# One period of 162 named steps, laid out in another order: a gated recurrent attention with a feed-forward layer on one core

## The chip, the core and the metric

The kernel runs on one core of a Trainium2 chip, in one launch. The metric is the device time of that launch in microseconds, from runs on the chip. A core has five engines with an instruction stream each, which run side by side and wait for one another by semaphores: PE (TensorE, matmuls into the accumulators called PSUM; its weight loads are listed apart, as PEld), DVE (VectorE), ACT (ScalarE), POOL (GpSimd) and SP (SyncE), which in this kernel only issues DMAs.

## The reference

There are two parts. The first is a gated linear attention, for 4 batches, 8 heads, 768 tokens and 40 channels a head; the loop over tokens carries a state C (40 by 40 per head), a row n and a running maximum m:

```
m_new = max(f[t] + m, i[t])
C = exp(f[t] + m - m_new) * C + exp(i[t] - m_new) * outer(v[t], k[t])
n = exp(f[t] + m - m_new) * n + exp(i[t] - m_new) * k[t]
y[t] = sigmoid(o[t]) * (C q[t]) / max(|n . q[t]|, 1)
```

The second part takes y as 3072 rows of 320 numbers: `h = x @ w_in` (320 to 2048), `g = max(h, 0) + alpha * min(h, 0)` with an alpha per channel, and `g @ w_out` (2048 to 320), all in float32.

## The kernel before, in words

**Tiling.** Tokens go in chunks of 128: six chunks a batch, 24 in all, called n = 0 to 23; c is a chunk's place in its batch, 0 to 5. Two chunks make a group g = n // 2 of 256 tokens, 12 groups, three to a batch. Inside a chunk the attention is done in matrix form: scores of keys against queries, times decays (exponentials of gate sums, masked to the lower triangle), times values; plus the queries times the state left by earlier chunks of the batch. The state of a batch starts anew with its chunk c = 0. Hence chunk c = 0 has no term from the state, and c = 5 makes no update.

**Precision.** Float32 results come from matmuls on parts. In attention, q, k, v, the decayed scores and the state are each cut into bfloat16 parts (a high part, the rest, the rest of the rest). ACT makes the high part, POOL or DVE subtracts it. The parts of q and k are then transposed by two DMAs (`th`, `ti`), and four more DMAs stack them (`sh`, `shifted`, lines 279 to 282). In the feed-forward layer x, w_in, g and w_out are each a high and a low part in the chip's fp32r format.

**The feed-forward layer of a group** (`FeedForward`, from line 675) has eight rounds fp = 0 to 7 of 256 hidden channels. A round has these steps, in capitals or small letters for two variants of the same work:

- V (or U): the up projection, 16 matmuls on PE (lines 697 to 704) into one of two PSUM buffers `ph`;
- r (R): the relu of the negated sum, on ACT (L707), into one of three buffers `g`;
- s (S): two operations of DVE (L712) that add the sum from PSUM; after them the `ph` buffer is free (in the U variant, which one round of eight uses, only after K);
- g (G): the high part `gh`, on ACT (L721); N: the low part `gl`, on POOL (K: on DVE) (L723). There are three buffers of each;
- D: the down projection, 12 matmuls on PE (L734) into `po`, the first eight on `gh`, the last four on `gl`.

F opens a group's layer, Z copies `po` out (DVE) and stores it (SP). Ahead of them X transposes the attention's output on PE into two PSUM tiles, and xa, xb (ACT) and xd, xe (DVE) cut it into parts; xe frees the second of the tiles.

**The steps of a chunk n of the later kind** (`late_steps`, from line 442):

- ld (q, k; L99), lv (v of a group; L112), lL (rows of gate sums; L119), lG (the output gate of a whole batch, six loads, line 128; issued at the last chunk of the batch before): loads on SP;
- ta to tg: parts of q and k. ta is a memset and two ACT copies; tb (L260, tile qr) and tc (L260, tile kr) are POOL's first subtractions; td, tf are ACT copies; te, tg (L265, tile Z) POOL's second. th, ti: the DMA transposes. sh: the four stacking DMAs;
- va, vb, vc, vd: parts of v, ACT and POOL in turn;
- e0, e1: the decays of the even and the odd heads, four ACT exponentials each, and POOL's mask (L436). s0, s1: the scores on PE (L462); m, c, d, h, l (0 or 1): the decayed scores and their parts, on DVE, ACT, DVE, ACT, DVE;
- y0, y1: times values on PE (L361), q0, q1 the sums on DVE. pi: queries times state on PE (L386), pt, ad the sum on DVE;
- r (three small operations of DVE), og (POOL, L418), xn (DVE, L420), xp (POOL): denominator, gate, output. oa (ACT, tanh, line 132) and ob (DVE) open the gate of the two chunks of a group;
- wd (POOL, L161): weighed keys. ua: outer products on PE (L183); ub (POOL, L210) and uc (DVE): the state's decay and sum; ud, ue, uf, ug: its parts, ACT and POOL in turn; uh (two DMAs, L233 and L234, that read the tile cw) and ui (one DMA, L236): the parts stacked.

The tiles qr, kr and cw share one tag with two buffers. So a tc may write only when an earlier cw is free, and that is when the DMAs of its uh have landed. The attention's PSUM tiles (scores, sums, pi, ua, X) share two tags with two buffers each, given out in turn.

**What sets the order.** Two lists of names do. `ORDER` (414 names) covers the first two groups up to the second one's middle, and `PATTERN` (162 names) is a period that `in_full` (line 650) repeats for g = -2 to 14. In it `s0.1` stands for s0 of chunk 2g + 1, `X:-1` for X of group g - 1, `V4<<` for round 4 of group g - 2's feed-forward and `V0<` for round 0 of group g - 1's. A name that doesn't exist (ua of a chunk with c = 5, say) or that was given out before is skipped. So in one period PE, ACT, DVE, POOL and SP do the attention of one group and the feed-forward of the groups before it, interleaved. `pin` (line 880) ties every instruction to the one before it on its engine. Each engine, and SP's queue of DMAs too, thus goes strictly by the list, and a step that waits holds up everything behind it on its engine.

Of the kernel before, what the change touches and what calls it, by code (L numbers as in the profile page):

```python
# [17 lines left out]
def kernel(ctx: ExitStack, tc: tile.TileContext, q, k, v, i_gate, f_gate, o_gate, w_in, w_out, alpha, out):  # L18
# [576 lines left out]
    def first_stacks():  # L595
# [40 lines left out]
        U12 fm5 ft5 o5h sc51 wg51 v5 o7d R12 S12 ta5 D10 G11 K11 o6s o6x gr5 og3 gg5 G12 gx5 gg4 D11 K12 D12 i30h i30l  # L636
        gx4 U13 gp5 D02 tp0 do3 U06 o7s gp4 o5l o6j vp0 R13 tp1 g05 S13 G13 N05 K13 o7x o6h D13 vp1 o7j U07 tp2 tp3
        R06 S06 R07 x4 x5 xa5 xd5 D03 D04 D05 S07 o7h o7l G06 K06 o6l D06 xa4 xd4 G07 K07 D07 Z0"""
    PATTERN = """va.1 uc.0 tf.1 V4<< c0.0 m1.0 N2<< d0.0 tg.1 r4<< V5<< r.-1 s4<< D2<< vc.0 g3<< th.1 og.-1 c1.0 h0.0 wd.1 xn.-1 r5<<
        xp.-1 d1.0 l0.0 g4<< ld.2 U6<< ud.0 h1.0 N3<< R6<< s5<< X:-1 N4<< g5<< S6<< lG.-1 ta.2 ua.1 V7<< ue.0 uf.0  # L640
        xa:-1 lL.2 xb:-1 l1.0 ub.1 vd.0 uc.1 r7<< N5<< tb.2 D3<< xd:-1 D4<< xe:-1 ti.1 F< ug.0 uh.0 G6<< sh.1 s7<<
        oa.0 y0.0 ld.3 pi.0 ob.0 tc.2 K6<< q0.0 y1.0 V0< td.2 e0.1 vb.1 vc.1 D5<< te.2 g7<< wd.2 q1.0 V1< pt.0 ad.0
        e1.1 r.0 s0.1 N7<< s1.1 r0< D6<< s0< vd.1 va.2 ud.1 tf.2 r1< m0.1 g0< c0.1 ue.1 tg.2 uf.1 lL.3 ug.1 m1.1 D7<<
        s1< d0.1 c1.1 og.0 th.2 g1< h0.1 ti.2 d1.1 ui.0 ta.3 xn.0 uh.1 V2< l0.1 ui.1 V3< sh.2 tb.3 Z<< r2< lG.8 h1.1
        N0< s2< l1.1 g2< D0< y0.1 N1< q0.1 y1.1 e0.2 pi.1 q1.1 vb.2 r3< tc.3 e1.2 lv.4 s1.2 xp.0 s0.2 td.3 ua.2 pt.1
        te.3 ad.1 s3< D1< ub.2 m0.2"""

    TWINS = dict(zip("UVRrSsGgKN", "VUrRsSgGNK"))

    def in_full():  # L650
# [4 lines left out]
        for g in range(-2, NG + 3):  # L655
            for x in PATTERN.split():
                if ":" in x:
# [645 lines left out]
```

## Time and profile before

| what | value |
|---|---|
| median of 3 runs | 478.0 us (477.29 to 484.12) |
| profiled execution | 480.86 us, span 479.1 us |
| busy share of the span | PE 98%, PEld 95%, DVE 65%, ACT 65%, POOL 64% |
| mean granted clock of TensorE | 0.986 of full |
| HBM | 36.90 MB read, 4.03 MB written |

The span runs from the first instruction of the profiled execution to its last; the time of the execution has about 1.8 us around it. An engine is busy while one of its instructions runs; matmuls overlap, so their ends are modelled. In rows of waits, `A <- B` says that A stood idle until B had ended. In names of tiles, `kS` and `qS` are the stacks of k and q, `pS` the scores, `pu` the outer products, `pH` values, `pI` queries times state, `ph` and `po` the up and down projections. `PEq` or `SPq` is the sequencer of an engine, which issues DMAs.

### The profile page before, as it was taken

The page shows a single profiled execution, that of the slowest core. Times are in us where ns is not written, and L with a number is a line of the kernel's source. Part 1 is how long each engine was busy: PE and PEld are TensorE (multiplying, and loading weights), DVE is VectorE, ACT ScalarE, POOL GpSimd, SP SyncE. Part 2 cuts the span into 40 slices and gives each one's busy share as a digit, 9 for nine tenths or more (in the row PEclk, how much of TensorE's full clock was granted, in tenths as well). Part 3 has the DMA queues.
Part 4 walks back from the last instruction along what each step waited for, and adds up shares of the span by engine and source line. Part 5 has one row for each costly group of instructions (what it writes and reads, how often), then busy time and mean ns, then how long its engine had stood idle before and what let it go on. Part 6 is the DMA issues. An engine that isn't in the chain of part 4 may idle for free.

```text
span 479.1 us, 11833 instructions
## 1 busy us (share of the span) xinstructions
PE 468.7 (98%) x4442; PEld 455.8 (95%) x4442; DVE 311.2 (65%) x664; ACT 312.5 (65%) x716; POOL 307.8 (64%) x395
## 2 busy tenths in 40 slices
PE   8999999999999999999989999999989999999997
PEld 6899989999999999999979999999989999999997
DVE  3869998658776676676556666766576676654221
ACT  4969898667766767666748758658657757523322
POOL 8531774844978868666977777677888776614231
PEclk9969999999999999999989999999999999999999
DMA  9979994959465565559685458559877533000000
GB/s 184 219 160 236 257 250 120 193 101 194 97 154 138 101 152 137 141 100 173 142 185 111 92 131 166 96 127 168 152 143 152 101 104 77 1 29 0 29 1 27
DMA packets 173922, 61.60 MB, mean 129 GB/s; under 512 B 140154, under 2 KB 166122, under 8 KB 173866
## 3 DMA queue, kind: packets, MB, share of 16 engines
q1 hardware_dynamic: 173786, 60.75, 60.0%
q8 instruction: 35, 0.57, 0.5%
q14 instruction: 21, 0.17, 0.1%
q10 hardware_dynamic: 80, 0.11, 0.1%
HBM read 36.90 MB, written 4.03 MB: 85 GB/s over the span
## 4 chain that ended last, share of the span: by engine, by line
PE 78%; DVE 5%; POOL 5%; SPq 3%; ACT 3%; DMA 3%; issue 2%; POOLq 0%; DVEq 0%; ACTq 0%
PE po L734 29%; PE ph L697 4%; PE ph L703 4%; PE ph L700 4%; PE ph L699 4%; PE ph L698 4%; PE ph L702 4%; PE ph L704 4%; PE ph L701 4%; PE pS L462 3%; PE pH L361 2%; PE pH L322 2%; PE pu L183 2%; PE p L551 2%; PE pS L1033 2%
## 5 line engine op out<-in xcount | busy, mean ns | idle before, releaser
L723 POOL TENSOR_TENSOR gl<-g,gh 128x512 fp32r<-128x512 f32 x77 | 100.2, 1306 | 43.3 <-ACT gh L721 37.6
L734 PE MATMUL po<-OH,gh 128*128 128x320 f32 x368 | 112.0, 316 | 0.0
L707 ACT ACTIVATE g<-ph 128x512 f32<-128x512 f32 x96 | 57.0, 594 | 82.7 <-PE ph L704 76.8
L734 PE MATMUL po<-OL,gh 128*128 128x320 f32 x368 | 109.7, 310 | 0.0
L712 DVE SCALAR_TENSOR_TENSOR g<-g,oma,ph 128x256 f32<-128x256 f32 x156 | 67.7, 476 | 52.0 <-ACT g L707 51.9
L734 PEld LDWEIGHTS po<-OH,gh 128*128 128x128 f32 x368 | 69.5, 189 | 0.4
L734 PEld LDWEIGHTS po<-OL,gh 128*128 128x128 f32 x368 | 69.5, 189 | 0.1
L734 PE MATMUL po<-OH,gl 128*128 128x320 f32 x368 | 69.0, 308 | 0.0
L734 PEld LDWEIGHTS po<-OH,gl 128*128 128x128 f32 x368 | 57.9, 188 | 0.0
L697 PE MATMUL ph<-XH,WH 128*128 128x256 f32 x192 | 56.4, 294 | 0.7 <-ACT wo L803 0.7
L436 POOL TENSOR_SCALAR_AFFINE_SELECT E<-E 128x512 f32<-128x512 f32 x40 | 25.6, 639 | 48.0 <-ACT E L433 47.6
L348 ACT CAST E<-pS 128x512 bf16<-128x512 f32 x72 | 41.1, 585 | 20.9 <-DVE pS L345 20.8
L703 PE MATMUL ph<-XL,WH 128*128 128x256 f32 x192 | 54.3, 283 | 0.0
L700 PE MATMUL ph<-XH,WL 128*128 128x256 f32 x192 | 54.2, 283 | 0.0
L699 PE MATMUL ph<-XH,WL 128*128 128x256 f32 x192 | 54.2, 282 | 0.0
L702 PE MATMUL ph<-XL,WH 128*128 128x256 f32 x192 | 54.2, 282 | 0.0
L721 ACT CAST gh<-g 128x512 fp32r<-128x512 f32 x77 | 47.5, 619 | 10.1 <-DVE g L712 6.9
L698 PE MATMUL ph<-XH,WH 128*128 128x256 f32 x192 | 54.2, 282 | 0.0
L701 PE MATMUL ph<-X,W 128*128 128x256 f32 x192 | 53.5, 279 | 0.2 <-POOL W L829 0.2
L704 PE MATMUL ph<-X2L,W 128*128 128x256 f32 x192 | 53.4, 278 | 0.0
L433 ACT ACTIVATE E<-Lb,bT 128x128 f32<-128x128 f32 x160 | 51.0, 392 | 0.0
L366 DVE TENSOR_REDUCE S<-pH 128x168 f32<-128x504 f32 x36 | 23.4, 679 | 22.3 <-PE pH L361 22.3
(193 smaller groups left out, 1141.9 us busy)
## 6 DMA issues: line engine op xcount, KB each, us to landing
Lb<-L_d SPq DMA_DIRECT2D x20, 512.0 KB
wo<-in_moe_w_out_dram SPq DMA_DIRECT2D x8, 640.0 KB
wi<-in_moe_w_in_dram SPq DMA_DIRECT2D x8, 512.0 KB
qn<-in_q_dram SPq DMA_DIRECT2D x24, 160.0 KB
kn<-in_k_dram SPq DMA_DIRECT2D x24, 160.0 KB
va<-in_v_dram SPq DMA_DIRECT2D x24, 160.0 KB
og<-in_o_gate_dram SPq DMA_DIRECT2D x24, 160.0 KB
out_dram<-ob SPq DMA_DIRECT2D x11, 320.0 KB
```

The lines of the kernel that those rows point to most:

```text
L697: nc.tensor.matmul(dst, WH[half][:, 0, hs], XH[:, 0], start=True, stop=False)
L698: nc.tensor.matmul(dst, WH[half][:, 1, hs], XH[:, 1], start=False, stop=False)
L699: nc.tensor.matmul(dst, WL[half][:, 0, hs], XH[:, 0], start=False, stop=False)
L700: nc.tensor.matmul(dst, WL[half][:, 1, hs], XH[:, 1], start=False, stop=False)
L701: nc.tensor.matmul(dst, W2[:, fs], X2, start=False, stop=False)
L702: nc.tensor.matmul(dst, WH[half][:, 0, hs], XL[:, 0], start=False, stop=False)
L703: nc.tensor.matmul(dst, WH[half][:, 1, hs], XL[:, 1], start=False, stop=False)
L704: nc.tensor.matmul(dst, W2[:, fs], X2L, start=False, stop=True)
L707: nc.scalar.activation(gt, ph, AF.Relu, scale=-1.0)
L712: nc.vector.scalar_tensor_tensor(out=y[:, e], in0=gt[:, e], scalar=oma[:, f : f + 1], in1=ph[:, e], op0=ALU.mult, op1=ALU.add)
L723: (nc.vector if split else nc.gpsimd).tensor_tensor(gl, y, gh.bitcast(F32), ALU.subtract)
L734: nc.tensor.matmul(po[j], x[:, e, j * P : (j + 1) * P], W[f // NB][:, f % NB], **ends)
```

## The change

The text of `PATTERN` is replaced. Both versions have 162 names. Eleven names are spelled with another group offset (for instance `ld.2`, `ld.3` are now `ld.4`, `ld.5`, and `ua.2` is `ua.0` of the next period), and over all periods both lists come to the same 1852 steps, each once. `ORDER` stays, so the first 414 steps are the same, in the same order. No operation, tile or buffer count changes.

```diff
--- before.py
+++ after.py
@@ -636,14 +636,14 @@
         U12 fm5 ft5 o5h sc51 wg51 v5 o7d R12 S12 ta5 D10 G11 K11 o6s o6x gr5 og3 gg5 G12 gx5 gg4 D11 K12 D12 i30h i30l
         gx4 U13 gp5 D02 tp0 do3 U06 o7s gp4 o5l o6j vp0 R13 tp1 g05 S13 G13 N05 K13 o7x o6h D13 vp1 o7j U07 tp2 tp3
         R06 S06 R07 x4 x5 xa5 xd5 D03 D04 D05 S07 o7h o7l G06 K06 o6l D06 xa4 xd4 G07 K07 D07 Z0"""
-    PATTERN = """va.1 uc.0 tf.1 V4<< c0.0 m1.0 N2<< d0.0 tg.1 r4<< V5<< r.-1 s4<< D2<< vc.0 g3<< th.1 og.-1 c1.0 h0.0 wd.1 xn.-1 r5<<
-        xp.-1 d1.0 l0.0 g4<< ld.2 U6<< ud.0 h1.0 N3<< R6<< s5<< X:-1 N4<< g5<< S6<< lG.-1 ta.2 ua.1 V7<< ue.0 uf.0
-        xa:-1 lL.2 xb:-1 l1.0 ub.1 vd.0 uc.1 r7<< N5<< tb.2 D3<< xd:-1 D4<< xe:-1 ti.1 F< ug.0 uh.0 G6<< sh.1 s7<<
-        oa.0 y0.0 ld.3 pi.0 ob.0 tc.2 K6<< q0.0 y1.0 V0< td.2 e0.1 vb.1 vc.1 D5<< te.2 g7<< wd.2 q1.0 V1< pt.0 ad.0
-        e1.1 r.0 s0.1 N7<< s1.1 r0< D6<< s0< vd.1 va.2 ud.1 tf.2 r1< m0.1 g0< c0.1 ue.1 tg.2 uf.1 lL.3 ug.1 m1.1 D7<<
-        s1< d0.1 c1.1 og.0 th.2 g1< h0.1 ti.2 d1.1 ui.0 ta.3 xn.0 uh.1 V2< l0.1 ui.1 V3< sh.2 tb.3 Z<< r2< lG.8 h1.1
-        N0< s2< l1.1 g2< D0< y0.1 N1< q0.1 y1.1 e0.2 pi.1 q1.1 vb.2 r3< tc.3 e1.2 lv.4 s1.2 xp.0 s0.2 td.3 ua.2 pt.1
-        te.3 ad.1 s3< D1< ub.2 m0.2"""
+    PATTERN = """og.-1 ua.0 m1.0 V4<< tf.1 ub.0 vb.1 xn.-1 V5<< tg.1 g2<< m0.0 N2<< vc.1 c1.0 r4<< vb.0 d1.0 xp.-1 th.1 h1.0 ti.1 uc.0
+        s4<< ud.0 D2<< ue.0 U6<< g4<< l1.0 g3<< N3<< uf.0 r5<< lG.-1 c0.0 vd.1 X:-1 vc.0 ua.1 lG.2 sh.1 ub.1 s5<< N4<<
+        oa.0 R6<< d0.0 g5<< ug.0 h0.0 l0.0 uc.1 V7<< N5<< xa:-1 vd.0 D3<< D4<< D5<< S6<< ta.2 tb.2 xb:-1 uh.0 lL.2
+        y0.0 xd:-1 pi.0 r7<< s7<< G6<< wd.2 tc.2 K6<< ob.0 xe:-1 q0.0 td.2 y1.0 F< q1.0 e0.1 te.2 V0< e1.1 tf.2 g7<<
+        ud.1 s0.1 r0< s1.1 V1< m0.1 s0< ui.0 c0.1 tg.2 m1.1 ta.3 c1.1 pt.0 d0.1 N7<< ad.0 D6<< ld.4 V2< D7<< th.2 d1.1
+        ue.1 g0< uf.1 tb.3 r1< h0.1 r.0 s1< V3< l0.1 og.0 ug.1 ti.2 uh.1 wd.3 tc.3 h1.1 lv.4 r2< e0.2 xn.0 sh.2 Z<<
+        l1.1 td.3 ui.1 pi.1 g1< s2< y0.1 N0< ld.5 xp.0 pt.1 e1.2 q0.1 r3< N1< y1.1 D0< q1.1 D1< s0.2 s1.2 va.3 ad.1
+        va.2 lL.3 te.3 r.1 s3<"""
 
     TWINS = dict(zip("UVRrSsGgKN", "VUrRsSgGNK"))
 
```

With names of one turn of batch (g = 6, chunks 12 and 13) the queues read as follows. A chunk's loads now stand two groups ahead.

```
SP before: th.13 ld.14 lG.11 lL.14 ti.13 uh.12 sh.13 ld.15 lL.15 th.14 ti.14 ui.12 uh.13 ui.13 sh.14 Z4 lv.16
SP after:  th.13 ti.13 lG.11 sh.13 uh.12 lL.14 ui.12 ld.16 th.14 ti.14 uh.13 lv.16 sh.14 Z4 ui.13 ld.17 lL.15
PE before: V44 V45 D42 U46 X:5 ua.13 V47 D43 D44 y0.12 y1.12 V50 D45 V51 s0.13 s1.13 D46 D47 V52 V53 D50 y0.13
           y1.13 pi.13 s1.14 s0.14 ua.14 D51
PE after:  ua.12 V44 V45 D42 U46 X:5 ua.13 V47 D43 D44 D45 y0.12 y1.12 V50 s0.13 s1.13 V51 D46 V52 D47 V53 pi.13
           y0.13 y1.13 D50 D51 s0.14 s1.14
POOL before: N42 tg.13 og.11 wd.13 xp.11 N43 N44 ta.14 ue.12 ub.13 vd.12 N45 tb.14 ug.12 tc.14 e0.13 vb.13 te.14
             wd.14 e1.13 N47 vd.13 ue.13 tg.14 ug.13 og.12 ta.15 tb.15 N50 N51 e0.14 vb.14 tc.15 e1.14 xp.12 te.15 ub.14
POOL after:  og.11 vb.13 tg.13 N42 vb.12 xp.11 ue.12 N43 vd.13 ub.13 N44 ug.12 N45 vd.12 ta.14 tb.14 wd.14 tc.14
             e0.13 te.14 e1.13 tg.14 ta.15 N47 ue.13 tb.15 og.12 ug.13 wd.15 tc.15 e0.14 N50 xp.12 e1.14 N51 te.15
```

## Rows read from the trace of the kernel before

**Rows 1.** The page's part 1: busy time of each engine, share of the span, instructions.

```profile
PE 468.7 (98%) x4442; PEld 455.8 (95%) x4442; DVE 311.2 (65%) x664; ACT 312.5 (65%) x716; POOL 307.8 (64%) x395
```

**Rows 2.** Waits of PE: engine, line, releaser: us in total, times, longest us.

```profile
PE pS L462 <- DMA kS<-kS: 4.0, 2, 2.2
```

**Rows 3.** Windows: us, busy (instructions) of PE, PEld, DVE, ACT, POOL, PEclk, DMA share, GB/s.

```profile
160.55:195.87 35.32, 35.32 (x362) 34.87 (x360) 24.12 (x52) 24.45 (x58) 27.23 (x36) 1.00 0.62 132
...
216.00:226.00 10.00, 10.00 (x107) 9.69 (x106) 6.39 (x15) 7.06 (x17) 6.51 (x8) 1.00 1.03 174
...
236.00:248.50 12.50, 10.32 (x120) 9.86 (x119) 8.45 (x18) 7.68 (x20) 10.97 (x15) 0.86 0.65 149
```

**Rows 4.** Chain of waits, 205 to 256 us: start us, us, what.

```profile
205.90 0.96 PE pH L361 x24
206.86 0.40 PE pI L386 x16
207.26 0.90 PE pS L462 x16
208.16 0.44 PE pu L183 x16
...
218.00 0.66 PE p L551 x6
...
244.85 1.74 PE pS L462 x16
...
247.31 2.48 PE po L734 x12
...
253.58 1.76 PE po L734 x12
```

**Rows 5.** Timeline of SP's queue, 212 to 250 us: start us, us, what it issues.

```profile
214.41 5.01 SPq L128 DMA_DIRECT2D og<-in_o_gate_dram  x6
...
220.20 3.34 SPq L269 DMA_TRANSPOSE kS<-Z  x1
223.64 0.78 SPq L233 DMA_DIRECT2D C<-cw  x1
...
225.34 0.59 SPq L279 DMA_DIRECT2D qS<-qS  x1
...
235.55 1.23 SPq L269 DMA_TRANSPOSE kS<-Z  x1
...
240.18 0.56 SPq L279 DMA_DIRECT2D qS<-qS  x1
...
243.62 1.67 SPq L112 DMA_DIRECT2D va<-in_v_dram  x2
```

**Rows 6.** Timeline of POOL there: start us, us, operation [idle before, releaser].

```profile
226.88 0.79 POOL L260 TENSOR_TENSOR kr<-kn,Z 128x320 f32<-128x320 f32 x1 [4.28 <-DMA C<-cw]
227.63 0.64 POOL L436 TENSOR_SCALAR_AFFINE_SELECT E<-E 128x512 f32<-128x512 f32 x1
...
234.72 0.80 POOL L265 TENSOR_TENSOR Z<-kr,Z 128x320 bf16<-128x320 f32 x1
```

**Rows 7.** Timeline of PE, a down projection just after scores: start us, us, matmul.

```profile
271.64 0.39 PE L734 MATMUL po<-OH,gh 128*128 128x320 f32 x1
271.87 0.31 PE L734 MATMUL po<-OL,gh 128*128 128x320 f32 x1
```

**Rows 8.** Groups by line: busy us, mean ns of one, idle before and releasers.

```profile
L723 POOL TENSOR_TENSOR gl<-g,gh 128x512 fp32r<-128x512 f32 x77 | 100.2, 1306 | 43.3 <-ACT gh L721 37.6 <-issue 3.9 <-POOL gl L723 0.6
...
L707 ACT ACTIVATE g<-ph 128x512 f32<-128x512 f32 x96 | 57.0, 594 | 82.7 <-PE ph L704 76.8 <-POOL gl L723 4.4 <-POOL cw L227 1.3
L712 DVE SCALAR_TENSOR_TENSOR g<-g,oma,ph 128x256 f32<-128x256 f32 x156 | 67.7, 476 | 52.0 <-ACT g L707 51.9
...
L345 DVE TENSOR_TENSOR pS<-pS,E 128x512 f32<-128x512 f32 x36 | 24.1, 695 | 16.1 <-PE pS L462 15.6 <-issue 0.2
...
L479 DVE TENSOR_TENSOR pI<-pI,S 128x336 f32<-128x336 f32 x15 | 7.7, 516 | 0.5
```

## The prediction

> **What bounds the kernel now.** First the page's busy times: PE 98%, every other engine 64 to 65% [rows 1]. Busy time of pipelined matmuls can hide slack, so I looked at windows next: from 160.55 to 195.87 us, one whole group, PE has no idle time at all (35.32 of 35.32) while POOL, the fullest of the rest, has 27.23 [rows 3]. Inside a batch the kernel is a gapless stream of matmuls, and an order of steps can't shorten that. So third, who made PE wait: scores (L462) for the K stacks' DMA, 2 times, 4.0 us in all, the longer one 2.2, hence 1.8 the other [rows 2]. Other waits of PE lie in the head, which isn't touched.
>
> Fourth, what the longer wait costs beyond itself. Between 236.00 and 248.50 the granted clock is 0.86 and PE busy 10.32 of 12.50 [rows 3]; the scores right after the wait take 1.74 us where 0.90 is normal [rows 4]. (1 - 0.86) x 12.5 = 1.75 us of full speed are lost: about 3.5 us at half clock. The two other windows stand at 1.00.
>
> Fifth, where that wait is from. Backwards: the stacks' copies (sh.14) start on SP at 240.18 and PE goes on at 244.85, so 4.67 from the first issue to the matmul [rows 4, 5]. They follow ti.14 at 235.55, which needs tg.14, a POOL operation ending at 235.5 [rows 5, 6]. POOL was late as kr (tc.14) stood 4.28 us for a DMA that reads the buffer it takes [rows 6]: uh.12, issued only at 223.64, behind ti.13 (3.34 us) and lG.11's six loads (5.01 us from 214.41) [rows 5]. After kr POOL did eight operations, with waits, before tg.14 was done: 8.6 us [rows 6].
>
> **The change, part by part.** All instructions stay; 162 names in the period stay; only orders per engine and queue change. Zero below is the start of V4 of the group at the turn (chunks 12, 13), as PE would run without gaps. An up step is (253.58 - 249.79) / 2 = 1.89 us, a down step 1.76, scores of a chunk 0.90, ua 0.44, both y 0.96, pi 0.40 [rows 4].
>
> *The turn.* In the new list ti.13 comes ahead of lG.11. POOL's queue then has og.11, vb.13 and tg.13 first, about 2.4 us at 0.80 each [rows 6]; ti.13 takes 1.23 to 3.34 [rows 5]; lG.11 starts at 3.6 to 5.7. Its rows give 5.01, sh.13 at most 3.44 (240.18 to 243.62), and 3.24 from uh.12's first issue to kr (223.64 to 226.88) [rows 5, 6]: kr is free at 15.3 to 17.4. POOL reaches kr after 17 operations, four of them gl at 1.31, the rest near 0.75 [rows 6, 8]: 15.0. So the wait is 0.3 to 2.4 instead of 4.28. Behind kr stand now only mask, Z, mask, Z (0.64 and 0.80 each) ahead of ti.14, no longer vb, te, wd, gl, vd and ue: tg.14 is done at 19 to 21. SP then issues ti.14 (1.23), uh.13 (1.70, from 223.64 to 225.34), lv.16 (1.67) and sh.14, which needs 4.67 to the matmul: 28 to 30.5. ui.12 and ui.13 are no longer in between. s0.14 is due at 35.3 less 0.90, 0.44 and the missing pi 0.40: 33.6. Spare 3 to 5 us, so both waits go: **-4.0**, and the dip with the first: **-1.75**.
>
> A rule on that dip. One wait of 2.2 drew the half clock, the one of 1.8 did not [rows 2, 3]. The Trainium skill (TensorE: Matmul & The Clock Gate, Part 1) says the array is throttled by default and activity releases it, so idling gives the clock back up. By that rule a wait near the limit need not have dipped in the timed runs; the saving would be 4.0 instead of 5.75. The trace agrees that idling precedes the fall; it has no second case.
>
> *One more switch.* PE leaves the FFN for attention four times a group now (X ua; y pi y; s s; y y pi s s ua) and five times in the new list (s0 s1 stand alone between V0 and V1, s s ua wrap round). The first down matmul behind scores takes 0.23 us to the next start [rows 7], one of a plain step 1.76 / 12 = 0.15 [rows 4]: 0.08 x 9 groups = **+0.7**.
>
> *Up steps and PSUM.* V2 must wait for s0 (two ph buffers). Between V0's end and V2 the list has now s0 s1, V1, D6: 0.90 + 1.89 + 1.76 = 4.55, where D5, V1, s0 s1, D6 and D7 made 8.1. The chain relu (0.59), m0.1 (0.70), two L712 (0.95) [rows 8] needs about 2.3. Covered by PE's own work; if DVE is over 2.2 us behind, V2 waits.
>
> *D0, D1 and POOL.* D0 and D1 now stand together behind y0 y1, and in POOL's order wd, kr and a mask are put ahead of N0. From V0's end: scores 0.45, then DVE m0, s0, m1, pt, d0, ad, d1, r: 0.70 + 0.95 + 0.70 + 0.52 + 0.70 + 0.52 + 0.70 + 0.52 (pt and r at the rate of ad's row) [rows 8], so r.0 at 5.8. POOL then og, ug, wd and kr at 0.80, mask 0.64, N0 1.31 [rows 6, 8]: 10.9; xp, mask, N1: 13.1 to 13.6. PE reads N0 at 0.90 + 3 x 1.89 + 2 x 1.76 + 1.36 + 1.17 (8 of 12 matmuls) = 12.6, N1 at 14.4. Spare 1.7 and 0.8. That is thin, but POOL's 27.2 of 35.3 let it catch up [rows 3]. Cost 0, bounds 0 and the cases below.
>
> *Earlier loads* (ld two groups ahead): same DMAs, off the path of sh; cost 0. *Tail and head*: the last group's up and down steps keep their order; 0.
>
> Sum: -4.0 - 1.75 + 0.7 = -5.05. The profiled execution took 480.86, its span 479.1; the median of the runs is 478.0, 2.9 below. 475.8 on the profiled scale, **473.0** on the runs'.
>
> **Rivals.** *The gate load waits (+).* oa.12 now stands eleven names behind lG.11; DMA share there is 1.03, the engines are full [rows 3]. If the tanh waits for its two slices only (two of six issues, about 1.7 us, and landing), ACT loses under 2 us and catches up. If for all six: they are issued by 3.6..5.7 + 5.01 and land no sooner than 1.5 later (225.34 to 226.88, rows 5 and 6), at 10 to 12. ACT then has nine operations of about 0.6 (relu's row) and DVE its K6 of about 0.7 ahead of V0's PSUM: 16.5 to 18.5. V0 is due at 4 ups, 4 downs, X 0.66, ua and two y [rows 4]: 16.7. PE waits 0 to 2 at two turns, perhaps with a dip of 1.75 each: up to +7.5, giving 473 to 480.5, 477 in the middle. For: the distance is short. Against: the code reads only two slices (lines 131, 132).
>
> *Nothing moves.* lG.11 still stands ahead of uh.12 and sh.13; if full DMA engines make sh.13 as slow as ti.13 was, kr is late as before: 478.7.
>
> *POOL falls behind in every group (slower).* Place: og.0 waits for r.0, N0 and N1 behind it, D0 and D1 next. It decides when r.0 is over 1.7 us later than summed; each us beyond is paid in nine groups. At 0.55 us a group the gain is gone; at 1.6 it is 2% slower: 487.6; with a dip of 1.75 in each, 490. For: POOL idles 2 to 3 us at og.0 and then has no pause. Against: 8 us idle a group [rows 3].
>
> *Weight loads are the measure.* From PE's rows the most to be had is 4.0 + 1.75. The Trainium skill (Perfetto Trace Analysis, opening note) would judge by weight-load busy time, not matmul busy time. That is 95%, so 23 us of room [rows 1], and a better packed order could take over 10 us: under 468. The window with PE 35.32 has weight loads 34.87 of it [rows 3], so hardly any such room lies where the change acts.
>
> **How the numbers follow.** Forecast 0.55 (472 to 476), gate load 0.20, nothing moves 0.07, POOL behind 0.16 (half of it over 2%), weight loads 0.02. 2%, 9.6 us, is about what a measurement of this kernel can tell from no change. Faster by that 0.02, slower 0.08, within 0.90. Low end: 478.0 less 5.75 less the 0.7 by which the fastest run lies under the median: 471.5. High end 480.5: gate load and nothing moves whole, the mild quarter of POOL behind; left out is about 0.15 above and 0.03 below.
>
> **What would show it.** Right: no PE wait on kS after 100 us; granted clock 1.00 from 40 us to the end; kr's wait under 2.5; tg to sh.14 done some us ahead of PE; groups of 35.3 us throughout. Wrong: PE or PEld waits on L723 (gl), L712 or L707 in each group; an ACT wait at L132 at two turns with PE idle behind; a fall of the clock in more places than one.

## The result, and the profile after

The changed kernel takes **474.23 us** (median of 20 runs, 471.48 to 481.9), the kernel before, run beside it, 479.08 (20 runs, 476.22 to 484.12). The ratio is **0.9881, 95% interval 0.9857 to 0.9905**: 5.7 us, or 1.2%, faster, and within the 2% that the forecast called "within". One run of after (481.9) and a few of before were disturbed, and the ratio leaves them out. The profiled execution of after took 475.88 us, its span 474.2, at a mean granted clock of 0.989 (before: 480.86, 479.1, 0.986).

I read the trace of after in the same order. First the page's busy times, which answer to [rows 1]:

```profile
PE 467.8 (99%) x4442; PEld 454.9 (96%) x4442; DVE 308.6 (65%) x664; ACT 314.8 (66%) x716; POOL 308.4 (65%) x395
```

The instruction counts are those of before, and the busy times are within 2.6 us. What is left of the difference is idle time and clock. Second, all waits of PE from 60 us to the end (engine, line, releaser: us in total, times, longest us):

```profile
PE ph L697 <- ACT wo L803: 0.7, 1, 0.7
PE ph L701 <- POOL W L829: 0.3, 1, 0.3
```

Both lie in the head, ahead of 90 us, and stand in before too (0.7 and 0.2). The row on kS [rows 2] is gone, and no other took its place. Third, windows of after (columns as in [rows 3]): a whole group inside a batch, the stretch that had the dip, and the whole group at the turn.

```profile
160.55:195.87 35.32, 35.32 (x361) 34.88 (x360) 23.91 (x53) 24.72 (x59) 26.35 (x34) 1.00 0.63 128
...
236.00:248.50 12.50, 12.50 (x146) 12.21 (x145) 8.69 (x21) 7.14 (x19) 11.47 (x15) 1.00 0.67 147
...
210.81:246.31 35.50, 35.50 (x362) 34.86 (x358) 23.85 (x53) 25.21 (x59) 28.13 (x37) 1.00 0.81 159
```

PE is busy for 12.50 of 12.50 where it was 10.32, the clock is 1.00 where it was 0.86, and the group at the turn runs without a gap. POOL has 28.13 busy of 35.50 there. It remains second.

Fourth, SP's queue at the turn (start us, us, what it issues), to be held against [rows 5]. Zero of the prediction, the start of V4, is 210.81 here.

```profile
210.31 1.23 SPq L269 DMA_TRANSPOSE kS<-Z  x1
211.67 4.31 SPq L128 DMA_DIRECT2D og<-in_o_gate_dram  x6
216.02 1.98 SPq L279 DMA_DIRECT2D qS<-qS  x1
...
220.35 0.71 SPq L233 DMA_DIRECT2D C<-cw  x1
221.11 0.82 SPq L234 DMA_DIRECT2D C<-cw  x1
221.97 0.49 SPq L119 DMA_DIRECT2D Lb<-L_d  x1
...
228.02 1.29 SPq L269 DMA_TRANSPOSE kS<-Z  x1
...
233.14 0.72 SPq L279 DMA_DIRECT2D qS<-qS  x1
```

The gate loads are out by 215.98, and uh.12 follows at 220.35 where it was 223.64. lL.14 (L119), the 512 KB of gate sums, now stands behind uh.12, not ahead. sh.14 starts at 233.14, 22.3 us after V4; before it was 29.8 (240.18, and V4 at 210.39). Fifth, POOL (columns as in [rows 6]):

```profile
224.12 0.79 POOL L260 TENSOR_TENSOR kr<-kn,Z 128x320 f32<-128x320 f32 x1
...
227.18 0.79 POOL L265 TENSOR_TENSOR Z<-kr,Z 128x320 bf16<-128x320 f32 x1
...
234.49 0.72 POOL L418 TENSOR_TENSOR og<-og,r 128x320 f32<-128x320 f32 x1 [1.41 <-DVE r L411]
...
238.89 1.29 POOL L723 TENSOR_TENSOR gl<-g,gh 128x512 fp32r<-128x512 f32 x1
...
240.94 1.28 POOL L723 TENSOR_TENSOR gl<-g,gh 128x512 fp32r<-128x512 f32 x1
```

kr has no bracket: it waits for nothing. The part Z that ti.14 needs is done 3.8 us after kr began, where it took 8.6.

Last, the starts of V4 of each group from the second steady one on, and the time to the next (us):

| group's V4 | before | after |
|---|---|---|
| 2 | 139.26, 35.95 | 139.65, 35.89 |
| 3 | 175.21, 35.18 | 175.54, 35.27 |
| 4 (turn) | 210.39, **39.24** | 210.81, 35.50 |
| 5 | 249.63, 35.80 | 246.31, 35.90 |
| 6 | 285.43, 35.19 | 282.21, 35.27 |
| 7 (turn) | 320.62, **37.42** | 317.48, 35.50 |
| 8 | 358.04, 35.91 | 352.98, 35.90 |
| 9 to 11 | 393.95, 63.62 | 388.88, 63.70 |

From the first row to the end of the last it is 318.31 before and 312.93 after: **-5.38 us**, of which 3.74 and 1.92 at the two turns, and nothing that can be told from the noise elsewhere. The head came out 0.66 us slower in this pair (V4 of the first steady group at 107.65 and 108.31), that first group takes 31.61 and 31.34 to the table's first row, and the tail from the table's end to the last matmul has 18.29 and 18.30.

### The profile page after: what moved, and what is told of

Same layout as the page of the kernel before. It is cut to its first block, busy times and chain, and to the rows that moved or that the text cites. A ratio compares the mean times of both kernels' runs of the same rounds, so it can differ in the third digit from the quotient of the medians.

```text
span 474.2 us, 11834 instructions
## 1 busy us (share of the span) xinstructions
PE 467.8 (99%) x4442; PEld 454.9 (96%) x4442; DVE 308.6 (65%) x664; ACT 314.8 (66%) x716; POOL 308.4 (65%) x395
## 4 chain that ended last, share of the span: by engine, by line
PE 89%; DVE 5%; POOL 2%; ACT 2%; issue 1%; POOLq 0%; DVEq 0%; ACTq 0%
PE po L734 35%; PE ph L697 5%; PE ph L703 4%; PE ph L700 4%; PE ph L698 4%; PE ph L699 4%; PE ph L702 4%; PE ph L704 4%; PE ph L701 4%; PE pH L361 4%; PE pS L462 3%; PE pH L322 2%; PE p L551 2%; PE pu L183 2%; PE pS L1033 1%; PE pI L386 1%
## 5 line engine op out<-in xcount | busy, mean ns | idle before, releaser
L734 PE MATMUL po<-OH,gh 128*128 128x320 f32 x368 | 110.7, 312 | 0.0
L697 PE MATMUL ph<-XH,WH 128*128 128x256 f32 x192 | 58.0, 302 | 0.7 <-ACT wo L803 0.7
L698 PE MATMUL ph<-XH,WH 128*128 128x256 f32 x192 | 54.1, 282 | 0.0
L348 ACT CAST E<-pS 128x512 bf16<-128x512 f32 x72 | 41.1, 581 | 15.9 <-DVE pS L345 15.3
L721 ACT CAST gh<-g 128x512 fp32r<-128x512 f32 x77 | 46.5, 618 | 7.2 <-DVE g L712 4.8
L433 ACT ACTIVATE E<-Lb,bT 128x128 f32<-128x128 f32 x160 | 50.0, 391 | 0.0
L345 DVE TENSOR_TENSOR pS<-pS,E 128x512 f32<-128x512 f32 x36 | 25.0, 696 | 31.1 <-PE pS L462 27.5
```

Of the source, the lines that this page charges most:

```text
L697: nc.tensor.matmul(dst, WH[half][:, 0, hs], XH[:, 0], start=True, stop=False)
L698: nc.tensor.matmul(dst, WH[half][:, 1, hs], XH[:, 1], start=False, stop=False)
L734: nc.tensor.matmul(po[j], x[:, e, j * P : (j + 1) * P], W[f // NB][:, f % NB], **ends)
```

## The experiments

All ratios are against the kernel before in the same series, unless said otherwise.

**What frees the turn?** The theory in the prediction was SP's order: ti and the gate loads lG stood ahead of uh, so kr came free late. Three kernels take the change apart; "old" and "new" name the list that is edited.

**1. Old list, ti ahead of lG**, so that all of SP's queue moves up, and nothing else.

```diff
- ... S6<< lG.-1 ta.2 ... D4<< xe:-1 ti.1 F< ug.0 uh.0 G6<< sh.1
+ ... S6<< ti.1 lG.-1 ta.2 ... D4<< xe:-1 F< ug.0 uh.0 G6<< sh.1
```

> The list of before with one name moved: ti.1 stands directly ahead of lG.-1, so SP issues the K transpose of chunk 13 ahead of the six gate loads. Theory (the gain lies at the two turns, and comes from the order of SP's queue and of POOL's): in the trace of before lG.11 starts at 214.41 and ti.13 takes 3.34 behind it; with ti.13 ahead at 1.2 to 1.3 us, uh.12 is issued some 3 us earlier than 223.64, the wait of kr falls from 4.28 to about 1, and the K stacks of chunk 14 come about 3 us earlier than 244.8, so PE's waits of 2.2 and 1.8 us go. Time 473 to 475 against 479 of before (ratio 0.988 to 0.992), PE waits on the K stacks 0. Rival A (POOL's order after kr is what matters): the wait of kr shrinks but tg.14 stays late behind vb, wd, gl and the rest, PE's waits fall by less than 1 us each, ratio 0.996 to 1.000. Rival B (the gain is spread over all groups): ratio 1.000.

Measured: 476.98 us (12 runs, 473.78 to 482.29), ratio 0.9951 (0.9913 to 0.9989). Its profiled execution took 482.29, with half clock for 10.24 us in the head and for 3.41 us behind each of two waits; I read its order and waits here and not its total. PE's waits for kS stayed, and so did POOL's for kr:

```profile
PE pS L462 <- DMA kS<-kS: 3.9, 3, 2.0
POOL kr L260 <- DMA C<-cw: 7.6, 2, 3.9
```

SP's queue and the kr at the first turn (V4 at 210.78):

```profile
214.81 4.60 SPq L128 DMA_DIRECT2D og<-in_o_gate_dram  x6
219.45 0.87 SPq L119 DMA_DIRECT2D Lb<-L_d  x1
220.42 0.78 SPq L233 DMA_DIRECT2D C<-cw  x1
```
```profile
226.73 0.80 POOL L260 TENSOR_TENSOR kr<-kn,Z 128x320 f32<-128x320 f32 x1 [3.74 <-DMA C<-cw]
```

uh.12 was issued 3.2 us earlier than before (220.42 for 223.64) and came hardly earlier: kr starts at 226.73 where it was 226.88, or 15.95 us after V4 where it was 16.49. From issue to kr it took 6.31 us in place of 3.24. The theory as I had put it, that the place in SP's queue decides, fell.

**2. Old list, tf and tg directly behind e1**, so that POOL does three operations fewer (N47, vd.13, ue.13) between kr and tg.14.

```diff
- e1.1 r.0 s0.1 N7<< s1.1 r0< D6<< s0< vd.1 va.2 ud.1 tf.2 r1< m0.1 g0< c0.1 ue.1 tg.2 uf.1
+ e1.1 tf.2 tg.2 r.0 s0.1 N7<< s1.1 r0< D6<< s0< vd.1 va.2 ud.1 r1< m0.1 g0< c0.1 ue.1 uf.1
```

> The list of before with tf.2 and tg.2 moved ahead, to directly behind e1.1, so POOL does the last part of chunk 14's keys before gl, vd and ue; SP's order stays, with ti.13 behind the gate loads. Theory: kr still waits about 4.3 us, but tg.14 is done about 2.5 us earlier than 235.5; ti.14 then starts at about 233.4, when th.14 is out, and the K stacks come 2.1 us earlier than 244.8. PE's first wait falls from 2.2 to about 0.1, the second from 1.85 to 0: ratio 0.988 to 0.992, while kr's waits stay. Rival A' (SP's order alone matters): PE's waits stay near 2, ratio 1.000. Rival B (spread over all groups): ratio 1.000.

Measured: 474.29 us (6 runs, 473.91 to 478.76), ratio 0.9898 (0.9857 to 0.9938). The wait of kr is as long as ever, but PE hardly waits:

```profile
PE pS L462 <- DMA kS<-kS: 0.9, 1, 0.9
PE pS L462 <- PE pI L386: 0.6, 1, 0.6
POOL kr L260 <- DMA C<-cw: 8.7, 2, 4.4
```
```profile
229.55 0.80 POOL L265 TENSOR_TENSOR Z<-kr,Z 128x320 bf16<-128x320 f32 x1
```

With V4 at 207.93, tg.14 is done 22.4 us after V4 in place of 25.1, and the clock stays at full speed behind both waits. So the half of the change that moves tg is nearly enough alone.

**3. New list, ti behind lG**, that is the order of before at this place.

```diff
- ... xp.-1 th.1 h1.0 ti.1 uc.0 ... uf.0 r5<< lG.-1 c0.0
+ ... xp.-1 th.1 h1.0 uc.0 ... uf.0 r5<< lG.-1 ti.1 c0.0
```

> The list of after with ti.1 put back directly behind lG.-1. Theory: ti.13 starts at about 216 instead of 210.3 and takes up to 3.3, uh.12 comes about 3 us later than 220.35, kr of chunk 14 waits about 2.5 us where it waited for nothing, and sh.14 starts about 3 us later than 233.1; PE needs it only at 244.9, some 7 us after it lands, so no wait of PE comes back: ratio to before as that of after, 0.985 to 0.991. Rival (the place of ti alone made the gain): PE waits for the K stacks at both turns again, about 2 us each, ratio 0.998 to 1.003.

Measured: 473.12 us (6 runs, 471.75 to 475.97), ratio 0.9861 (0.9825 to 0.9897), as fast as the new list. kr waits again, and PE doesn't notice:

```profile
POOL kr L260 <- DMA C<-cw: 3.8, 2, 1.9
```

```profile
234.22 0.74 SPq L282 DMA_DIRECT2D kS<-kS  x1
```
```profile
242.08 1.07 PE L462 MATMUL pS<-qS,kS 120*128 120x128 bf16 x16
```

sh.14 was issued by 234.96 and its scores began at 242.08, 7.1 us later; in after it is 8.7 (236.13 and 244.88). The new list has slack at the turn, and ti's place uses up 1.6 us of it.

**What holds uh up?** In the first experiment lG (six loads) and lL.14 (512 KB) stood right ahead of uh.12. From 212 to 218 us the DMA share is 0.98 there, from 218 to 224 it is 1.13. So the data ahead of uh may count, not the issue.

**4. Experiment 1, and lL moved behind sh.**

```diff
- ... xa:-1 lL.2 xb:-1 ... F< ug.0 uh.0 G6<< sh.1 s7<<
+ ... xa:-1 xb:-1 ... F< ug.0 uh.0 G6<< sh.1 lL.2 s7<<
```

> The list of before with ti.1 directly ahead of lG.-1 (as in the run that moved it alone) and with lL.2, the 512 KB of gate sums for chunk 14, moved from ahead of uh.0 to behind sh.1. With ti moved alone, uh.12 was issued 3.2 us earlier (220.4 instead of 223.6) but kr still waited 3.7 us, so its DMAs landed no earlier: something ahead of them held the DMA engines, whose share stood near 1 from 212 to 224 us. Theory G (the six gate loads do): kr's wait stays at 3 or more, PE's waits stay between 1.5 and 2, ratio 0.994 to 1.000. Theory L (the 512 KB do, which were issued right ahead of uh.12): kr's wait falls to about 1.2, PE's waits to 0, ratio 0.987 to 0.992.

Measured: 472.12 us (4 runs, 471.78 to 476.2), ratio 0.9889 (0.9823 to 0.9954).

```profile
PE pS L462 <- DMA kS<-kS: 0.8, 2, 0.5
POOL kr L260 <- DMA C<-cw: 1.0, 1, 1.0
```
```profile
216.11 0.78 SPq L233 DMA_DIRECT2D C<-cw  x1
```
```profile
219.48 0.80 POOL L260 TENSOR_TENSOR kr<-kn,Z 128x320 f32<-128x320 f32 x1
```

uh.12, issued at 216.11, let kr go by 219.48: at most 3.4 us, against 6.31 with lL.14 ahead. The 512 KB were in the way, in the DMA engines and not in SP's queue. The packets in the traces show it: in experiment 1 those of lG.11 (160 bytes each) run until 221.59, those of lL.14 (512 bytes) from 221.18 to 224.99, and those of uh.12 (672 bytes) only from 222.99 to 225.99; here lG.11's run until 218.01 and uh.12's from 217.56 to 218.83. Of PE's two waits left, 0.5 us lies at 132.91, in the group ahead of the table's rows, and 0.2 at the last turn.

**5. Old list, one of the six gate loads** of batches 2 and 3; the other five are left out, and the tile keeps what it held.

```diff
-        if c0 == 0:
+        if c0 == 0 and b < 2:
             o_tiles[b] = sb.tile([P, NC, H, D], F32, tag="og", name=f"og{b}", bufs=1)
+        elif c0 == 0:
+            o_tiles[b], c1 = o_tiles[b - 1], 1
```

> The list of before; of the output gate of batches 2 and 3 only the first of six chunks is loaded (the other five are left out, the tile's earlier content stands in for them), so lG costs SP one issue and the DMA engines a sixth. Theory G (the gate loads hold the DMA engines, and so uh's landing): kr's wait goes to 0 or nearly, the K stacks of chunk 14 come 4 us earlier, PE's waits at the turns are 0, ratio 0.986 to 0.991. Theory L (the 512 KB of lL.14): kr still waits 2 to 3, PE's waits are about 1. Rival (POOL's long queue behind kr alone): PE's waits stay at 1.5 to 2.

Measured: 474.84 us (10 runs, 471.36 to 476.13), ratio 0.9928 (0.9890 to 0.9966). kr does not wait, and PE has no wait for kS; two waits of the scores for pi are left:

```profile
PE pS L464 <- PE pI L388: 0.5, 2, 0.3
```
```profile
217.69 0.78 SPq L235 DMA_DIRECT2D C<-cw  x1
```

So leaving out gate loads frees uh too. But it takes time out of SP's queue as well as data out of the DMA engines: uh.12 is issued 6.5 us after V4 (211.18) and not 13.3, and its packets run until 222.19, 4.5 us after that issue, with ti.13 and lL.14 just ahead. How much of the backlog in before is the gate loads' is not shown by it.

**The turns in all these profiles** (V4 to V4 in us; the last column from V4 of group 2 to the end of the table above):

| kernel | group 4 | group 7 | all |
|---|---|---|---|
| before | 39.24 | 37.42 | 318.31 |
| after | 35.50 | 35.50 | 312.93 |
| 1, ti ahead | 38.68 | 39.11 | 319.16 |
| 2, tg ahead | 36.25 | 36.65 | 314.29 |
| 3, new list, ti behind | 35.50 | 35.50 | 312.94 |
| 4, ti ahead, lL behind | 35.41 | 35.80 | 312.71 |
| 5, one gate load | 35.42 | 35.87 | 313.07 |

These times leave the head out, whose clock moves the medians by as much as the experiments differ. Once its turns are cleared (4 and 5), the old list takes what the new one takes. So the gain lies at the turns, and none of it is spread over the other groups.

**How thin is POOL's cover of D0 and D1?** The rival on the slow side hung on this. In the new list, in five groups, POOL does its weighing of the keys (wd of chunks 9, 13, 15, 19, 21), which lies ahead of N0 and N1, several times over, with the same result.

```diff
+        for _ in range(4 if n > 7 and n % GC == 1 else 1):
             (nc.gpsimd if n in KDP else nc.vector).tensor_tensor(
```

**6. Four times (+2.2 us).**

> The list of after, with POOL's wd of chunks 9, 13, 15, 19 and 21 done four times over, to the same result: 3 x 0.72 = 2.2 us more of POOL in five groups, in the queue directly ahead of N0 and N1. It measures the spare of POOL ahead of the two down steps D0, D1, which was summed at 1.7 and 0.8 us. From the trace of after: N0 is done at 240.18 and read at about 242.4, N1 at 242.23 and read at 244.3, and POOL idles 0.5 between; so 2.2 us more leave both just in time. Theory (spare 2.3 and 2.0 plus the idle 0.5): PE waits 0 to 0.3 us a group, time as after. Rival (the summed spare of 0.8 holds): PE waits about 1.4 us in each of five groups, +7 us.

Measured: 473.09 us (1 run). PE waits for nothing after 90 us.

**7. Seven times (+4.3 us).**

> As the run with 2.2 us more, but 6 x 0.72 = 4.3 us more of POOL in the same five groups. Theory: N0 is done 1.6 us after PE wants it and N1 a little later still, PE waits 1.6 to 2 us in each of the five groups, +8 to +10 us on after, and more if the granted clock falls with a wait: so the rival of the prediction that ends slower has its place here and decides at about 2.5 us. Rival (POOL's idle time elsewhere takes it): PE waits under 0.5 us a group, time as after.

Measured: 488.32 us (1 run). First the waits of PE; then the granted clock in 40 slices, in tenths of full speed; then the windows around the third wait and around the second:

```profile
PE po L735 <- POOL gl L724: 7.9, 5, 1.8
```
```profile
PEclk9969999999999999999989999999989999999999
```
```profile
247.00:252.00 5.00, 4.10 (x18) 4.00 (x19) 0.88 (x2) 2.21 (x5) 5.00 (x8) 0.66 0.58 142
209.00:215.00 6.00, 4.90 (x54) 4.39 (x55) 2.36 (x8) 2.89 (x7) 6.00 (x9) 1.00 0.66 148
```

The down projection waits in all five groups, 1.30 or 1.78 us. From V4 to V4 these groups take 1.8 to 2.3 us more than after's, with 1.70 for a dip taken off where there is one, which is more than the waits listed. The added 4.3 less that leaves 2.0 to 2.5 us as the spare; the trace of after says 2.3 and 2.1 (below). Twice, at 248.08 and 360.72, a dip of 3.41 us at half clock follows. The mechanism of that rival is real and each microsecond beyond the spare is paid in each group, as it was priced; the dip came in two of the five groups and not in each. Its point lies beyond what the change uses.

**Why do the runs of one kernel differ by 4 us?** In after's trace the granted clock is 0.50 from 24.35 to 34.59 us, in the head, and nowhere else. Going by the mean granted clock of 31 of the 32 runs of after (20, and 12 of experiment 10; the one of 481.9 also has 0.989, and the clock does not explain it):

| mean clock | us |
|---|---|
| 0.999 to 1.000 | 471.5 to 472.2 |
| 0.996 | 473.0 to 473.7 |
| 0.993 | 474.7 |
| 0.989 | 475.1 to 476.3 |

Ahead of that stretch PE is listed as busy without a gap, on narrow matmuls: the window from 17 us on, and the largest two of its groups (shapes, count, busy us and mean ns, idle before):

```profile
17.00:24.35 7.35, 7.35 (x63) 6.65 (x62) 5.72 (x14) 7.30 (x18) 4.72 (x5) 1.00 1.12 214
```
```profile
L1033 PE MATMUL pS<-qf,kf 104*128 104x128 f32 x16 | 2.0, 277 | 0.0
L322 PE MATMUL pH<-va,E 128*128 128x42 f32 x16 | 2.0, 285 | 0.0
```

The kernel has a list FILL of dense matmuls put ahead of the values of early chunks.

**8 and 9. New list, 12 more of these fillers.** The second is the same kernel again in a later series.

```diff
-    FILL = {3: 4, 4: 14, 5: 4}
+    FILL = {0: 6, 1: 6, 3: 4, 4: 14, 5: 4}
```

> The list of after with FILL = {0: 6, 1: 6, 3: 4, 4: 14, 5: 4}: six more dense bfloat16 matmuls of 256 columns ahead of the values of chunks 0 and 1, at about 21 and 25.5 us. Runs of after differ by the granted clock: 1.0 goes with 471.5 to 471.9 us, 0.996 with about 473.2, 0.989 with 475.1 to 475.9; the profile shows the half clock between 24 and 35 us, right behind the matmuls of 42 columns at 20 to 24. Theory H (the thin work of the head drops the clock): all runs near clock 1.0, median 471.5 to 473, ratio to before 0.982 to 0.987. Rival (the head's PE time is the bound and the extra work of about 1.3 us is simply added): 475 to 476.5, clock as before, ratio 0.991 to 0.995.

> The kernel of after with six dense matmuls more ahead of the values of chunks 0 and 1, again. If the fill holds the clock in the head (theory H), all runs stand within 472 to 473.5 at a clock of 0.999 or 1.0, and the median is 1 to 2 us under that of the kernel of after on this chip. Rival (the first five runs were luck): the same spread of the clock, median 474 to 475.

**10. After, unchanged, beside it.**

> The kernel of after, unchanged, on the same chip and beside the same runs as the one with more fill, to compare the two. Its runs should spread over 471.5 to 476 us with the granted clock between 1.0 and 0.989; ratio to before 0.986 to 0.991; no wait of PE after 100 us.

**11. 22 more fillers** (`{0: 12, 1: 10, ...}`).

> The list of after with FILL = {0: 12, 1: 10, 3: 4, 4: 14, 5: 4}, twice the added fill of the run with six each. Theory H (thin work drops the clock in the head): clock 1.0 in nearly all runs, the extra work costs 1 to 2 us of PE time, median 472 to 474. Rival (PE's time in the head is the bound): 476 to 478.

Measured: with 12 more fillers 472.41 us (5 runs, 472.21 to 473.23; ratio 0.9841, 0.9811 to 0.9870) and again 472.39 (6 runs, 471.82 to 473.59; 0.9878, 0.983 to 0.9927); after beside the second 473.17 (12 runs, 471.47 to 476.29; 0.9896, 0.9858 to 0.9934); with 22 more fillers 473.09 (6 runs, 472.73 to 473.82; 0.9901, 0.9864 to 0.9938). The head, after and then the 12 more fillers, second series:

```profile
24.35:34.59 10.24, 10.24 (x54) 9.39 (x53) 7.17 (x15) 6.33 (x17) 2.44 (x4) 0.50 0.85 176
```
```profile
24.35:34.59 10.24, 9.68 (x90) 8.63 (x89) 9.22 (x22) 8.17 (x23) 4.78 (x6) 1.00 0.84 182
```

In the same 10.24 us PE gets through 90 matmuls in place of 54. All 17 runs with more fillers have a mean clock of 0.999 or 1.000, of after's 9 of 32. They save the 3.7 us of the slowest heads and cost some tenths in the best. On the median that is 0.8 us under after in the same series, and the intervals overlap: the fillers make the runs even (1.8 us from end to end in place of 4.8); that they make the kernel faster on the median is not shown. That kernel is the evenest of this study; experiment 4's median, 472.12 in 4 runs, is as low.

## Why the prediction was right

**Bound and size.** Forecast 473.0 from 478.0, hence -5.05; measured -5.7 on the ratio, -5.38 in the two traces behind the head. On the profiled scale 475.8 was forecast and 475.88 came, with a head 0.66 us slower; so close a hit is luck, with runs that spread over 4 us by their clock. The median of before had itself been a little low: 479.08 in the 20 runs, and 479.08 less 5.05 is 474.0 against the 474.23 measured.

**The two waits, -4.0: right.** [rows 2] is gone. **The dip, -1.75: right in the trace, smaller in the runs.** The half-clock stretch of before measured 3.41 us, so 1.70 lost, in its profiled execution:

```profile
245.03:248.44 3.41, 3.41 (x36) 3.13 (x34) 1.67 (x4) 0.58 (x1) 3.02 (x4) 0.50 1.08 189
```

Four runs of before in the experiments' series had a mean clock of 1.000, so no dip at all, and took 474.47, 474.71, 474.83 and 477.11; after at 1.000 took 471.5 to 471.9. There the gain is 2.6 to 5.6, mostly near 3, so without the dip. Over all runs with a clock on record, 51 of before and 32 of after, time times mean clock (which takes the half-clock stretches out) has the medians 474.7 and 471.2. That is 3.5 us, about the waits less the switches. The clock itself costs 0.9 us less on average, or 1.6 with the longest runs taken in, and not 1.75. The doubt that the prediction had on this term was in place. One of its reasons was not: it said that the trace has no second case of a fall. The same trace has one in the head, where no gap precedes it:

```profile
17.00:23.16 6.16, 6.16 (x54) 5.67 (x54) 4.79 (x11) 6.14 (x16) 3.60 (x5) 1.00 1.01 171
23.16:33.40 10.24, 10.24 (x55) 8.97 (x54) 7.06 (x17) 6.04 (x14) 2.42 (x3) 0.50 0.97 217
```

**The switch, +0.7: mis-sized.** The waits and the dip, 4.0 and 1.70, are 5.7 gone; the stretch shrank by 5.38. That leaves about +0.35 for nine groups, 0.04 a group and not 0.08: groups 3 and 6 take 35.27 where they took 35.18 and 35.19, the others run from 0.06 less to 0.10 more. I had charged the first matmul behind a change at its full distance to the next, though both lists also have runs of steps in which the following matmul makes part of it good; this part of the reason is argued, not shown.

**The turn's times: right in order, several us too late.** From V4's start:

| step | forecast | measured |
|---|---|---|
| lG.11 starts | 3.6 to 5.7 | 0.9 |
| sh.13, issue to issue's end | at most 3.44 | 4.23 |
| kr free, POOL there | 15.3 to 17.4, 15.0 | by 13.3, 13.3 |
| tg.14 done | 19 to 21 | 17.2 |
| K stacks there (sh.14's first issue + 4.67) | 28 to 30.5 | 27.0 |
| s0.14 | 33.6 | 34.1 |

The rows of PE for D0, D1 and s0.14:

```profile
241.27 0.39 PE L734 MATMUL po<-OH,gh 128*128 128x320 f32 x1
...
243.11 0.31 PE L734 MATMUL po<-OH,gh 128*128 128x320 f32 x1
...
244.88 1.07 PE L462 MATMUL pS<-qS,kS 120*128 120x128 bf16 x16
```

The miss that the others follow from is the first. I let POOL begin og, vb and tg at V4's start; in fact POOL runs ahead of PE there, and tg.13 was done at 210.28, before V4. So the spare is 7.1 us, not 3 to 5: the misses fell on the safe side. sh.13 was the one slower step, its first copy (1.98 us) standing right behind the gate loads.

**Why kr came free: the mechanism was put too simply.** The prediction took 3.24 us from uh's issue to kr as a fixed price and made SP's order the cause. Experiment 1 shows that the price is 6.31 when uh is issued earlier with lG and lL.14 right ahead. It held in after (kr was free 3.77 us after uh's first issue at the latest), and the new list also puts lL.14 behind uh.12, a move that I had left out of the sum. That this move is why it held is argued from experiments 1 and 4; no run has the new list with lL.14 ahead. For the price of 3.24 it was luck that the list made the move. And experiment 2 shows that the second thing, tg.14 drawn up behind kr, nearly does it alone (0.9 and 0.6 us of waits are left), and experiment 4 shows the same of an early kr (0.8 us left). The list does both, and undoing ti's place (experiment 3) costs nothing.

**ph and PSUM: right.** No wait of PE on ph inside a batch. **D0, D1 and POOL: right, a little better than summed.** From V0's end (229.75) r.0 was done at +4.7 (5.8 forecast), N0 at +10.4 (10.9), N1 at +12.5 (13.1 to 13.6). The down steps began at 241.27 and 243.11 and reach gl 1.17 later, so the spare is 2.3 and 2.1 where 1.7 and 0.8 were summed. Experiments 6 and 7 confirm it from both sides. The 490 that the prediction gives for a dip in each group does not come out of its terms: 473.0 and nine times 1.6 and 1.75 make 503.

**The gate load rival did not come.** oa.12 ran at 217.34, 1.4 us after the last gate load was issued (215.98) and with no idle time of ACT ahead of it. The gate's packets in the trace run from 212.85 to 219.18, so the tanh did not stand for all six:

```profile
217.34 0.74 ACT L132 ACTIVATE og<-og 128x640 f32<-128x640 f32 x1
```

**Nothing moves:** excluded by the trace: kr does not wait. **Weight loads as the measure:** their share went from 95 to 96%, and the kernel gained what PE's own gaps had held, not the 23 us beside the weight loads.

## What to carry to other kernels

Where an engine is gapless inside a period, an order is worth what the few waits at the seams cost, and the sum of these rows was the gain to within half a microsecond. A small DMA that frees a buffer is late for what is already in the DMA engines, not only for its place in the issuing queue: move bulk loads behind it, and look for the second queue (here POOL's eight operations behind kr) that turns a late buffer into a late result. Where a kernel's median hangs on its clock, compare one group's length in each trace. Before calling an order thin, add work at the suspected place until something waits; that gives the spare in microseconds.

## What the runs showed of the hardware

**Landing times are those of the backlog.** uh's two DMAs took 3.24 us from first issue to the waiting reader in before, 6.31 in experiment 1 with six gate loads and 512 KB just ahead, at most 3.4 in experiment 4 with the gate loads ahead and the 512 KB behind.

**A wait of 1.6 to 2.2 us may or may not be followed by half clock.** Before: the wait of 2.2 was, that of 1.8 was not. Experiment 1: gaps of 1.61 and 2.04 both were. Experiment 7: of three gaps of 1.78 two were, of two of 1.30 none. Experiment 2: 0.6 and 0.9 were not. The stretches behind these waits were 3.41 us long each.

**The clock falls without a wait, too.** In after's head PE is listed as busy throughout, on narrow matmuls, and still the granted clock goes to 1.2 GHz for 10.24 us in some executions (in the profiles of experiments 2, 3 and 6, with the same head, for 3.41 us, in that of experiment 4 not at all); with twelve dense bfloat16 matmuls more the mean clock was 0.999 or 1.000 in all 11 runs, so 2.4 GHz. The Trainium skill (TensorE: Matmul & The Clock Gate, Part 1) says that activity releases the throttle. The trace agrees in that more matmuls there kept the clock up, but its busy time does not tell when the clock falls: the stretch at half clock is listed as 10.24 busy of 10.24, and what ran ahead of it as 7.35 of 7.35.
